# Exponentials of an attention block on GpSimd: one block of 256 per unit by a power, beside VectorE's polynomial

## The chip, the core and the metric

The kernel runs on one core of a Trainium2 chip. The metric is the device time of one execution in microseconds (us); the median of three runs before the change is 932.26 us (931.24 to 934.92). TensorE (PE) multiplies matrices, ScalarE (ACT) evaluates functions, VectorE (DVE) does arithmetic on tiles, GpSimd (POOL) is a slower processor for tiles, and SyncE (SP) issues most DMAs.

## What is computed

```
x = A_x                                           # 1 x 2048 x 1024, bf16
g = sigmoid((x * gate_w).sum(-1))
a = 2 Re(C h) + x * Dskip,   h_t = Lam_bar h_(t-1) + B_bar x_t      # 1024 complex states, 2048 steps
q, k, v = x @ wqkv                                # 32 heads of 32
b = softmax(q k^T / sqrt(32)) v @ wo              # no mask, 2048 x 2048 scores a head
out = g * a + (1 - g) * b
```

## The kernel before, in words

**The attention loop sets the order of all work.** The 32 heads go in 8 groups of four, the 2048 queries in 8 blocks of 256; a group with a block is a *unit* (64 in all, g and qb of `normalize`, L1707). A unit has 8 *bursts*, each of which takes two tiles of 128 keys. So there are 512 bursts, counted by p in the loop of `build` (L1781). A burst has 8 score matmuls (L1615), which fill two slots of two PSUM banks (128 x 1024 scores each), and two exponentials, one for each slot (`exp` in `burst`, L1626). The probabilities lie in the tiles `pt` (and, early, in others that are free: the names f_cT, f_OT, f_Et in the profile) and are multiplied with V some bursts later (`pv`, L1684: 16 matmuls of 33 columns a burst, all accumulated in one PSUM bank with a column of ones, which gives the sum of the softmax). At the end of a unit `normalize` takes the reciprocal of the sums and scales.

**Everything else is fitted into the gaps by a planner that runs when the program is built.** Each burst has a place for four dense matmuls of 512 columns (`MM_PER_PERIOD`, L1847 on): projections for the next group (`d_qk`, `d_v`), the input of the state-space part (`d_u`), its output (`d_c`) and the output projection (`d_out`). They go through PSUM bank 7, and VectorE empties it (`evac`) after each chain of eight or so. VectorE's own work stands in lists: tables (`table_ops`), the folding of C (`fold_ops`) and, above all, the 32 items of the recurrence (`item_ops`, L1335: products, two scans of 512 steps, products). The planner holds a model of VectorE's clock, `dve_t`, adds to it a fixed price for each operation (0.61 us for a product, 1.24 for a scan, 0.735 for a step of the polynomial) and puts an operation into a burst if it ends in time. The order of every engine's queue is fixed by this; at run time only semaphores hold things back, and each engine takes its queue in order.

**The polynomial.** ScalarE alone would do 16 exponentials of 1024 columns a unit. For the bursts named in `X_PLAN` and `X_AT` (L935, L936), 256 of the 2048 exponentials of a burst (head 4 of the second key tile, the last 256 columns of the second slot) are done on VectorE instead: `x_in` (L1624) scales the scores from PSUM into `xi` as whole numbers, and the second exponential of that burst, which waits for it (`deps=[first]`, L1632), then has 768 columns (L1631). Two such blocks make a *pair*: when the second is in, three operations on 512 columns evaluate the polynomial (`x_ops`, L1658, L1659, L1655), GpSimd turns the result into the bits of a bf16 (L1656) into `xp`, and `x_pv` (L1667) multiplies it with V, 7 or 9 bursts after the start of the unit. With two pairs a unit, four of its eight bursts have a short exponential. Before the change this is so from burst 112 (unit 14) to 507, but for bursts 320 to 327 and 332 to 351.

GpSimd has little else: for each item it copies the last state (`hl`, L1358, behind the second scan), and three times it carries the state over (`carry`, L1385).

**Buffers.** `wb` holds the weights of two groups for q, k and v and three tiles of B; the `wo` rows come into the same places when these are no longer used.

Of the kernel before, what the change touches and what calls it, by code (L numbers as in the profile page):

```python
# [6 lines left out]
BF = mybir.dt.bfloat16  # L7
# [926 lines left out]

X_AT = ((0, 2), (4, 6))  # L935
X_PLAN = (112, 116, 120, 124, 128, 132, 136, 140, 144, 148, 152, 156, 160, 164, 168, 172, 176, 180, 184, 188, 192, 196, 200, 204, 208, 212, 216, 220, 224, 228, 232, 236, 240, 244, 248, 252, 256, 260, 264, 268, 272, 276, 280, 284, 288, 292, 296, 300, 304, 308, 312, 316, 328, 352, 356, 360, 364, 368, 372, 376, 380, 384, 388, 392, 396, 400, 404, 408, 412, 416, 420, 424, 428, 432, 436, 440, 444, 448, 452, 456, 460, 464, 468, 472, 476, 480, 484, 488, 492, 496, 500, 504)  # L936
X_COLS = 256
# [21 lines left out]
class FastPath:  # L959

    def __init__(self, nc, S, es, d, flag):
# [10 lines left out]
        self.V = T("V", [128, 2, 16, 4, 33], BF)  # L972
        wb = T("wb", [128, 9216], BF)
        self.w = wb[:, 0:6144].rearrange("p (s q a n) -> p s q a n", s=2, q=3, a=8)
        self.bT = wb[:, 6144:9216].rearrange("p (s a n) -> p s a n", s=3, a=8)

        row = lambda o, n: wb[:, o:o + 1024 * n].rearrange("p (a n) -> p a n", a=n)
        self.wo3 = [row(0, 3), row(6144, 3), row(3072, 1), self.cT[0][:, 0:1, :]]
        self.wo = [(self.wo3[0][:, a, :], "wo0") for a in range(3)] + [(self.wo3[1][:, a, :], "wo1") for a in range(3)]
        self.wo += [(self.wo3[3][:, 0, :], "wo3"), (self.wo3[2][:, 0, :], "wo2")]  # L980
# [4 lines left out]
        self.hp = hp  # L985
        self.hpx = wb[:, 6144:9216].rearrange("p (k n) -> p k n", k=6)
        ub = T("ub", [128, 2, 2, 512], BF)
# [70 lines left out]
    def ld_x(self, i, eng="sp"):  # L1058

        for r, n in ((0, 128), (1, 128)) if i == 0 else ((2 * i, 256),):  # L1060
            self.dma(lambda e, r=r, n=n: e.dma_start_transpose(self.xT[:, :, 128 * r:128 * r + n], self.x2[128 * r:128 * r + n, :]),  # L1061
                     [], [("xr", r + k) for k in range(n // 128)], "ld_x", eng)

    def ld_w(self, g, part, eng="sp"):
        cb = 1024 * part + 128 * g
        self.dma(lambda e: e.dma_start(self.w[:, g % 2, part], self.wsrc[:, :, cb:cb + 128]), [], [("w", g % 2, part)], "ld_w", eng)

# [12 lines left out]
    def begin(self):  # L1080
# [24 lines left out]
        pool(lambda e: e.tensor_copy(flat(24, 28), ioti), ["ioti"], ["iot"])  # L1105
        pool(lambda e: e.tensor_scalar(flat(28, 32), flat(24, 28), 16.0, 0.0, ALU.mult, ALU.add), ["iot"], ["ioth"])
        pool(lambda e: e.memset(self.V[:, :, :, :, 32:33], 1.0), [], ["v1"])
        pool(lambda e: e.memset(self.init[:], 0.0), [], ["init"])
# [13 lines left out]
    def piece(self, part, i, bank, first):  # L1122

        ps, w, xT = self.ps, self.w, self.xT
        for h in range(2):
            r = 2 * i + h

            def mm(e, r=r, h=h):
                m = None
                for a in range(8):  # L1130
                    m = e.matmul(ps[:, bank, 128 * h:128 * (h + 1)], w[:, 0, part, a, :], xT[:, a, 128 * r:128 * (r + 1)], start=(a == 0), stop=(a == 7))
                return m
            kw = dict(writes=[("bank", bank)]) if h == 0 else dict(acc=[("bank", bank)])
            yield lambda mm=mm, kw=kw, r=r: self.S.op("pe", mm, reads=[("w", 0, part), ("xr", r)], name="proj", **kw)

    def half256(self, part, i, half):
        ps, w, xT = self.ps, self.w, self.xT

        def mm(e):
            m = None  # L1140
            for a in range(4 * half, 4 * half + 4):
                m = e.matmul(ps[:, 7, 0:256], w[:, 0, part, a, :], xT[:, a, 256 * i:256 * (i + 1)], start=(a == 0), stop=(a == 7))
            return m
        self.S.op("pe", mm, reads=[("w", 0, part), ("xr", 2 * i), ("xr", 2 * i + 1)], name="proj", **(dict(acc=[("bank", 7)]) if half else dict(writes=[("bank", 7)])))

    def opening(self):
        S, ps, w, xT, dve = self.S, self.ps, self.w, self.xT, self.dve

# [265 lines left out]
    def d_qk(self, g, part, ch, bank=7):  # L1414
        ps, w, xT = self.ps, self.w, self.xT
        mms = []
        for a in range(8):
            mms.append((1, lambda e, f, l, a=a: e.matmul(ps[:, bank, :], w[:, g % 2, part, a, :], xT[:, a, 512 * ch:512 * (ch + 1)], start=f, stop=l),  # L1418
                        [("w", g % 2, part)] + self.xtok(ch)))
        if part == 0:  # L1420
            z = (4 * g + ch) % 5
            dst, tok = self.Q[:, z, :], ("Q", z)
        else:
            dst, tok = self.K[:, g % 2, 512 * ch:512 * (ch + 1)], ("K", g % 2, ch)
        return self.chain(mms, "proj", lambda: self.dve(lambda e: e.tensor_copy(dst, ps[:, bank, :]), [("bank", bank)], [tok], "evac_qk"), bank)  # L1425

    def d_v(self, g, f, bank=7):
        ps, w, xT = self.ps, self.w, self.xT
        mms = []
        for q in range(4):  # L1430
            kt = 4 * f + q
            for half in range(2):
                def fn(e, first, last, q=q, kt=kt, half=half):
                    m = None
                    for a in range(4 * half, 4 * half + 4):
                        m = e.matmul(ps[:, bank, 128 * q:128 * (q + 1)], xT[:, a, 128 * kt:128 * (kt + 1)], w[:, g % 2, 2, a, :],  # L1436
                                     start=(a == 0), stop=(a == 7))
                    return m
                mms.append((1, fn, [("w", g % 2, 2)] + self.xtok(f)))
        src = ps[:, bank, :].rearrange("p (k h c) -> p k h c", k=4, h=4)  # L1440
# [162 lines left out]
    def burst(self, B):  # L1603
# [17 lines left out]
        if mine is not None:  # L1621
            b, n = mine
            s = sl[1]
            first = self.dve(lambda e: e.tensor_scalar(self.xi[:, X_COLS * n:X_COLS * (n + 1)], ps[:, 2 * s + 1, 512 - X_COLS:512], X_A, X_LO, ALU.mult, ALU.max),  # L1624
                             [("S", s)], [("xi", n)], "x_in")
        def exp(z):  # L1626
            s, p = sl[z], self.pt_of(B, z)
# [16 lines left out]
    def x_ops(self, b):  # L1644
# [8 lines left out]
        def last():  # L1653
# [6 lines left out]
                (X_LAST, 0.0, last)]  # L1660

    def x_flush(self):
        c, wait, f = self.xbg.pop(0)
# [20 lines left out]
    def pv(self, q0, q1):  # L1684

        ps, V = self.ps, self.V
        for q in range(q0, q1):
# [6 lines left out]
            def mm(e, B=B, z=z, p=p, kl=kl, i=i, g=g):  # L1694
                m = None
                for h2 in range(1 if z == kl == 1 and B in self.x_of else 2):
                    for qt in range(2):
# [27 lines left out]
    def build(self):  # L1725
# [8 lines left out]
        for m in range(3):  # L1734
            self.ld_b(m)
        for part in (1, 2, 0):
            self.ld_w(1, part)
        self.plan()
        self.pt_own = {}
        self.x_of, self.x_batch, self.x_when = {}, [], {}  # L1740
        self.xbg, self.x_done, self.x_out = [], set(), 0
        self.opening()
# [38 lines left out]
        for p in range(first, NBURST):  # L1781
# [10 lines left out]
            period = PERIOD - (0.17 if p - 1 in self.x_of else 0.0)  # L1792
            if p in self.x_of:
# [28 lines left out]
            if pg == 25 and g + 2 < GROUPS:  # L1822
                assert g or not (proj[0] or cur and cur.tag == "proj")
                for part in (1, 2, 0):
                    self.ld_w(g + 2, part)
            wsv = self.d["B_wo"].rearrange("(a p) n -> p a n", p=128)
            if p == 386:
                self.dma(lambda e: e.dma_start(self.wo3[0], wsv[:, 0:3, :]), [], ["wo0"] + [("w", 0, q) for q in range(3)], "ld_wo")
            if not cs and cur is None and not wo1 and self.c_left[3] == 0:
                wo1 = True  # L1830
                self.dma(lambda e: e.dma_start(self.wo3[1], wsv[:, 3:6, :]), [], ["wo1"] + [("bT", r) for r in range(3)] + [("hp", 8, k) for k in range(6)], "ld_wo")
            if g >= 6 and not wo6 and not cs and self.c_left[3] == 0:
                wo6 = True
                self.dma(lambda e: e.dma_start(self.wo3[3], wsv[:, 6:7, :]), [], ["wo3", ("cT", 0, 0), ("cTf", 0, 0, 0), ("cTf", 0, 0, 1)], "ld_wo")
            if g >= 6 and not last and not proj[7] and not us and not cs and cur is None and not self.bg:

                last = True
                xs = [("xr", r) for r in range(16)]
                assert wo1 and wo6
                self.dma(lambda e: e.dma_start(self.wo3[2], wsv[:, 7:8, :]), [], ["wo2"] + [("w", 1, q) for q in range(3)] + xs, "ld_wo")  # L1840
            if g >= 6 and not cs and self.c_left[3] == 0 and nal < 8 and p > self.c_end:
# [280 lines left out]
```

## Time and profile before

| | us |
|---|---|
| median of 3 runs | 932.26 |
| lowest, highest | 931.24, 934.92 |
| the profiled execution, own time | 928.48 |
| its span in the profile | 926.7 |
| ACT busy in the span | 908.3 (98%) |
| PE busy | 883.7 (95%) |
| DVE busy | 758.9 (82%) |
| POOL busy | 74.4 (8%) |

The span lies within the execution's own time: 1.8 us are outside of it. The page of the profile gives busy times, a strip of 40 slices of the span (a digit is the busy share in tenths), the chain of work that ended last, and groups of instructions: line, engine, operation, written tile <- read tiles, shapes, how often, the busy time in us, the mean duration of one in ns, and then the idle time of the engine just before them. A window of the trace gives for each engine its busy time and in brackets the number of instructions that touch the window. A timeline gives the start in us, the time, and the instruction; xN stands for N in a row.

### The profile page before, as it was taken

The numbers are of one execution on the slowest core, as the hardware profiler recorded it, in microseconds if no ns is written. First come the engines' busy times: TensorE is split into PE (matmuls) and PEld (weight loads), VectorE is DVE, ScalarE is ACT, GpSimd is POOL, SyncE is SP. The second block draws the span as 40 slices with busy tenths as digits, with TensorE's granted clock in tenths as the row PEclk, the third lists the DMA queues.
The fourth block names the chain that finished last, engine by engine and source line by source line (L and its number), as shares of the span: only waits on it lengthen the run. The fifth ranks groups of instructions, "written<-read, shape, count | busy, mean of one in ns | idle before, by whom it ended". The sixth has DMA issues, their size and how long they took to land.

```text
span 926.7 us, 33866 instructions
## 1 busy us (share of the span) xinstructions
PE 883.7 (95%) x15095; PEld 502.8 (54%) x15316; DVE 758.9 (82%) x1310; ACT 908.3 (98%) x1034; POOL 74.4 (8%) x156
## 2 busy tenths in 40 slices
PE   8899999999999999999999999999999999989995
PEld 4555744447555565556655565555655655545553
DVE  2789989888989989889898989998998655676665
ACT  6999999999999999999999999999999999999997
POOL 2000000000100100102110100100010010001000
PEclk9999999999999999999999999999999999999999
DMA  9579737730114305572011511523002012424312
GB/s 205 93 127 167 115 80 137 156 86 16 42 53 102 70 20 102 120 160 52 19 51 53 122 38 27 120 64 102 19 17 65 21 48 74 145 85 123 118 63 75
DMA packets 170920, 77.71 MB, mean 84 GB/s; under 512 B 147216, under 2 KB 155408, under 8 KB 170768
## 3 DMA queue, kind: packets, MB, share of 16 engines
q1 hardware_dynamic: 168608, 74.94, 35.9%
q8 instruction: 121, 1.98, 0.9%
q10 hardware_dynamic: 2160, 0.53, 0.3%
q14 instruction: 31, 0.25, 0.1%
HBM read 25.18 MB, written 20.97 MB: 50 GB/s over the span
## 4 chain that ended last, share of the span: by engine, by line
PE 51%; ACT 36%; DVE 8%; issue 2%; DMA 1%; SPq 1%; DVEq 0%; ACTq 0%
ACT f_pt L1634 28%; PE f_ps L1700 11%; PE f_ps L1615 11%; PE f_ps L1495 8%; PE f_ps L1418 8%; PE f_ps L1448 6%; PE f_ps L1436 5%; ACT f_pt L1631 4%; DVE f_xi L1624 3%; ACT f_cT L1634 2%; ACT f_OT L1634 1%; ACT f_Et L1634 1%; SPq L1061 1%; PE f_ps L1679 1%; DMA f_xT<-in_A_x_dram 1%
## 5 line engine op out<-in xcount | busy, mean ns | idle before, releaser
L1634 ACT ACTIVATE f_pt<-f_ps 128x1024 bf16<-128x1024 f32 x760 | 727.7, 1113 | 1.2 <-PE f_ps L1615 1.0
L1700 PEld LDWEIGHTS f_ps<-f_V,f_pt 128*128 128x128 bf16 x7184 | 222.4, 96 | 94.8 <-issue 67.5
L1700 PE MATMUL f_ps<-f_V,f_pt 128*128 128x33 bf16 x7184 | 257.9, 178 | 0.3 <-ACT f_pt L1634 0.3
L1615 PE MATMUL f_ps<-f_Q,f_K 32*128 32x256 bf16 x4096 | 203.4, 273 | 14.4 <-ACT f_pt L1634 5.6
L1631 ACT ACTIVATE f_pt<-f_ps 128x768 bf16<-128x768 f32 x184 | 162.8, 885 | 3.0 <-DVE f_xi L1624 1.6
L1615 PEld LDWEIGHTS f_ps<-f_Q,f_K 32*128 32x128 bf16 x4096 | 60.8, 92 | 152.3 <-ACT f_pt L1634 125.4
L1448 PE MATMUL f_ps<-f_xT,f_wb 128*128 128x512 bf16 x448 | 117.7, 379 | 7.9 <-issue 2.3
L1418 PE MATMUL f_ps<-f_xT,f_wb 128*128 128x512 bf16 x406 | 106.7, 379 | 4.2 <-DVE f_K L1425 0.3
L1656 POOL TENSOR_SCALAR f_xp<-f_xq 128x512 int16<-128x512 f32 x92 | 57.3, 623 | 603.5 <-DVE f_xq L1655 385.9
L1624 DVE TENSOR_SCALAR f_xi<-f_ps 128x256 int32<-128x256 f32 x184 | 77.7, 423 | 19.5 <-PE f_ps L1615 13.7
L1355 DVE TENSOR_TENSOR_SCAN f_ht<-f_pf,f_init,f_ut 128x512 bf16<-128x512 f32 x64 | 79.7, 1272 | 0.0
L1495 PE MATMUL f_ps<-f_cT,f_hp 128*128 128x512 bf16 x240 | 67.6, 379 | 2.1
L1658 DVE SCALAR_TENSOR_TENSOR f_xq<-f_xi 128x512 f32<-128x512 uint16 x92 | 63.7, 692 | 3.1
L1659 DVE SCALAR_TENSOR_TENSOR f_xq<-f_xq,f_xi 128x512 f32<-128x512 f32 x92 | 63.6, 692 | 3.1
L1655 DVE SCALAR_TENSOR_TENSOR f_xq<-f_xi,f_xq 128x512 f32<-128x512 int16 x92 | 63.6, 691 | 2.7
L1448 PEld LDWEIGHTS f_ps<-f_xT,f_wb 128*128 128x128 bf16 x512 | 40.0, 96 | 40.6 <-issue 8.6
L1436 PE MATMUL f_ps<-f_wb,f_xT 128*128 128x128 bf16 x896 | 59.3, 219 | 0.0
L1526 PE MATMUL f_ps<-f_wb,f_OT 128*128 128x512 bf16 x186 | 55.0, 379 | 2.9 <-DVE f_Et L1538 0.9
L1418 PEld LDWEIGHTS f_ps<-f_xT,f_wb 128*128 128x128 bf16 x464 | 36.1, 96 | 35.4 <-issue 7.6
L1452 DVE CAST f_ub<-f_ps 128x512 bf16<-128x512 f32 x64 | 44.1, 689 | 11.8 <-PE f_ps L1448 9.2
L1436 PEld LDWEIGHTS f_ps<-f_wb,f_xT 128*128 128x128 bf16 x896 | 50.4, 97 | 3.8 <-issue 3.8
L1713 DVE RECIPROCAL f_rc<-f_ps 128x8 f32<-128x8 f32 x63 | 13.1, 207 | 44.2 <-PE f_ps L1679 35.7
(149 smaller groups left out, 797.7 us busy)
## 6 DMA issues: line engine op xcount, KB each, us to landing
u_scratch<-f_ub SPq DMA_DIRECT2D x64, 128.0 KB, 2.0
f_ub<-u_scratch SPq DMA_DIRECT2D x32, 256.0 KB, 2.8
ag_scratch<-f_Ag SPq DMA_DIRECT2D x32, 256.0 KB, 2.0
f_hp<-ag_scratch SPq DMA_DIRECT2D x32, 256.0 KB, 3.0
f_wb<-in_B_wqkv_dram SPq DMA_DIRECT2D x21, 256.0 KB, 4.2
out_dram<-f_xT SPq DMA_DIRECT2D x16, 256.0 KB, 2.0
f_wb<-in_B_wo_dram SPq DMA_DIRECT2D x2, 768.0 KB
f_OT<-f_On SPq DMA_TRANSPOSE x63, 2.3
```

Of the source, the lines that this page charges most:

```text
L1355: ops.append((1.24, lambda ri=ri: dve(lambda e: e.tensor_tensor_scan(ht[:, ri, :], rr, ut[:, ri, :], self.init[:, ri, j:j + 1], ALU.mult, ...
L1418: mms.append((1, lambda e, f, l, a=a: e.matmul(ps[:, bank, :], w[:, g % 2, part, a, :], xT[:, a, 512 * ch:512 * (ch + 1)], start=f, stop=l ...
L1436: m = e.matmul(ps[:, bank, 128 * q:128 * (q + 1)], xT[:, a, 128 * kt:128 * (kt + 1)], w[:, g % 2, 2, a, :], start=(a == 0), stop=(a == 7))
L1448: mms.append((1, lambda e, f, l, a=a: e.matmul(ps[:, 7, :], bT[:, (2 * n + ri) % 3, a, :], xT[:, a, 512 * ch:512 * (ch + 1)], start=f, sto ...
L1495: mms.append((1, lambda e, f, l, j=j, ri=ri, h=h: e.matmul(ps[:, 7, :], h[:, cols], cT[ri][:, j, 512 * cb:512 * (cb + 1)], start=f, stop=l ...
L1615: m = e.matmul(ps[:, 2 * sl[h // 2] + h % 2, 256 * kl:256 * (kl + 1)], K[32 * h:32 * h + 32, g % 2, 128 * kt:128 * (kt + 1)], Q[32 * h:32 ...
L1624: first = self.dve(lambda e: e.tensor_scalar(self.xi[:, X_COLS * n:X_COLS * (n + 1)], ps[:, 2 * s + 1, 512 - X_COLS:512], X_A, X_LO, ALU.m ...
L1631: self.S.op("act", lambda e: e.activation(flat(self.tile[p]), flat(ps[:, 2 * s:2 * s + 2, :]), ACT.Exp, scale=SCALE), reads=[("S", s)], wr ...
L1634: self.act(lambda e: e.activation(self.tile[p], ps[:, 2 * s:2 * s + 2, :], ACT.Exp, scale=SCALE), [("S", s)], [("pt", p)], "exp")
L1655: self.dve(lambda e: e.scalar_tensor_tensor(xq[:], hi, 128.0 / X_K, xq[:], ALU.mult, ALU.add), i2 + ["xq"], ["xq"], "x_q")
L1658: return [(0.73, 0.0, lambda: self.dve(lambda e: e.scalar_tensor_tensor(xq[:], lo, E2 / E3 * w, lo, ALU.add, ALU.mult), i2, ["xq"], "x_q") ...
L1700: m = e.matmul(ps[:, 6, o:o + 33], self.tile[p][:, h2, 256 * kl + 128 * qt:256 * kl + 128 * (qt + 1)], V[:, g % 2, 2 * i + kl, h, :], star ...
```

## The change

For units 8 to 49 (bursts 64 to 399) a unit has one polynomial pair, at its bursts 2 and 4, and one block of a new kind, at its burst 0. Units 50 to 63 keep two pairs. So units 8 to 13, which had none, now have three short exponentials each, and most of the units from 14 to 49 have three where they had four. The number of blocks goes from 184 to 42 + 138 = 180.

For the new block VectorE copies the 256 scores of each partition from PSUM, scaled to the base 2 and held above -126, as f32 into `yf` (`y_in`; the second exponential of the burst waits for it, and then has 768 columns). GpSimd raises 2 to these powers in four instructions of 64 columns (`y_pow`, tensor_tensor with a broadcast column of twos), which are put into its queue at bursts 0, 2, 4 and 6 of the unit. All four need only `yf`; the next unit's `y_in` needs all four to have read it. The result `yp` has two places, and `y_pv` multiplies it with V nine bursts after the start of the unit, ahead of the second exponential of that burst.

To find room in SBUF for `yf` and `yp`, the weights for q have one place for all groups instead of two: their load moves from the place pg 25 of the group before the last to pg 28 of the group before, and their four projections come at pg 32 or later. The rows of `wo` are spread over five loads instead of four.

```diff
-X_AT = ((0, 2), (4, 6))
-X_PLAN = (112, 116, 120, 124,
...
+X_AT = ((0, 2), (4, 6), (2, 4))
+Y_COLS = 64
+Y_PLAN = (64, 72, 80, 88, 96,
...
+X_PLAN = (64, 72, 80, 88, 96,
...
-        wb = T("wb", [128, 9216], BF)
+        wb = T("wb", [128, 8192], BF)
+        self.wq = wb[:, 0:1024].rearrange("p (a n) -> p a n", a=8)
...
+        self.yf = T("yf", [128, X_COLS], F32)
+        self.yp = T("yp", [128, 2, X_COLS], BF)
...
+        if B in self.y_of:
+            s = sl[1]
+            first = self.dve(lambda e: e.tensor_scalar(self.yf[:], ps[:, 2 * s + 1, 512 - X_COLS:512], SCALE * math.log2(math.e), -126.0, ALU.mult, ALU.max),
+                             [("S", s)], ["yf"], "y_in")
...
+    def y_pow(self, s, k):
+        cols = slice(Y_COLS * k, Y_COLS * (k + 1))
+        self.pool(lambda e: e.tensor_tensor(self.yp[:, s, cols], self.pf[:, 33, 0:1].to_broadcast([128, Y_COLS]), self.yf[:, cols], ALU.pow),
+                  ["yf", "two"], [("yp", s, k)], "y_pow")
+
+    def y_pv(self, B):
+
+        ps, V = self.ps, self.V
+        U, i = divmod(B, BURSTS)
+        g = U // QUNITS
+
+        def mm(e):
+            m = None
+            for qt in range(2):
+                o = 33 * (4 * qt + 3)
+                m = e.matmul(ps[:, 6, o:o + 33], self.yp[:, U % 2, 128 * qt:128 * (qt + 1)], V[:, g % 2, 2 * i + 1, 3, :],
+                             start=False, stop=False, skip_group_check=True)
+            return m
+        self.S.op("pe", mm, reads=[("yp", U % 2, k) for k in range(X_COLS // Y_COLS)] + [("V", g % 2, i // 2), "v1"], acc=["O"], name="pvy")
...
-                proj[g][8 + c].after = 16 * c
+                proj[g][8 + c].after = max(16 * c, 32)
...
+            if p in Y_PLAN:
+                self.y_of.add(p)
             if p % 4 == 0 and p in X_PLAN:
-                self.x_plan(p // 8, X_AT[p // 4 % 2])
+                self.x_plan(p // 8, X_AT[2 if p in Y_PLAN else p // 4 % 2])
...
+            if p in self.y_of:
+                self.dve_t = max(self.dve_t, t0 + 0.45) + 0.4
+            if p % 8 // 2 * 2 * Y_COLS < 2 * X_COLS and p % 2 == 0 and p // 8 * 8 in self.y_of:
+                self.y_pow(p // 8 % 2, p % 8 // 2)
...
+                if p % 8 == 1 and p - 9 in self.y_of:
+                    self.y_pv(p - 9)
                 second()
...
+            if pg == 28 and g + 1 < GROUPS:
+                assert not (cur and cur.tag == "proj")
+                self.ld_w(g + 1, 0)
```

More of the change, by code (lines that the diff above doesn't have):

```diff
@@ L972, in __init__ @@
         self.V = T("V", [128, 2, 16, 4, 33], BF)
-        wb = T("wb", [128, 9216], BF)
-        self.w = wb[:, 0:6144].rearrange("p (s q a n) -> p s q a n", s=2, q=3, a=8)
-        self.bT = wb[:, 6144:9216].rearrange("p (s a n) -> p s a n", s=3, a=8)
+        wb = T("wb", [128, 8192], BF)
+        self.wq = wb[:, 0:1024].rearrange("p (a n) -> p a n", a=8)
+        self.wkv = wb[:, 1024:5120].rearrange("p (s q a n) -> p s q a n", s=2, q=2, a=8)
+        self.bT = wb[:, 5120:8192].rearrange("p (s a n) -> p s a n", s=3, a=8)
         row = lambda o, n: wb[:, o:o + 1024 * n].rearrange("p (a n) -> p a n", a=n)
-        self.wo3 = [row(0, 3), row(6144, 3), row(3072, 1), self.cT[0][:, 0:1, :]]
-        self.wo = [(self.wo3[0][:, a, :], "wo0") for a in range(3)] + [(self.wo3[1][:, a, :], "wo1") for a in range(3)]
+        self.wo3 = [row(1024, 2), row(5120, 3), row(3072, 1), self.cT[0][:, 0:1, :], self.cT[0][:, 1:2, :]]
+        self.wo = [(self.wo3[0][:, a, :], "wo0") for a in range(2)] + [(self.wo3[4][:, 0, :], "wo4")] + [(self.wo3[1][:, a, :], "wo1") for a in range(3)]
         self.wo += [(self.wo3[3][:, 0, :], "wo3"), (self.wo3[2][:, 0, :], "wo2")]
@@ L1062, in ld_x, with w_of @@
                      [], [("xr", r + k) for k in range(n // 128)], "ld_x", eng)
+    def w_of(self, g, part):
+        return (self.wkv[:, g % 2, part - 1], ("w", g % 2, part)) if part else (self.wq, ("w", 0, 0))
     def ld_w(self, g, part, eng="sp"):
         cb = 1024 * part + 128 * g
-        self.dma(lambda e: e.dma_start(self.w[:, g % 2, part], self.wsrc[:, :, cb:cb + 128]), [], [("w", g % 2, part)], "ld_w", eng)
+        w, tok = self.w_of(g, part)
+        self.dma(lambda e: e.dma_start(w, self.wsrc[:, :, cb:cb + 128]), [], [tok], "ld_w", eng)
     def ld_b(self, m):
@@ L1106, in begin @@
         pool(lambda e: e.tensor_scalar(flat(28, 32), flat(24, 28), 16.0, 0.0, ALU.mult, ALU.add), ["iot"], ["ioth"])
+        pool(lambda e: e.memset(self.pf[:, 33, 0:1], 2.0), [], ["two"])
         pool(lambda e: e.memset(self.V[:, :, :, :, 32:33], 1.0), [], ["v1"])
@@ L1122, in piece @@
     def piece(self, part, i, bank, first):
-        ps, w, xT = self.ps, self.w, self.xT
+        ps, xT = self.ps, self.xT
+        w = self.w_of(0, part)[0]
         for h in range(2):
@@ L1130, in mm @@
                 for a in range(8):
-                    m = e.matmul(ps[:, bank, 128 * h:128 * (h + 1)], w[:, 0, part, a, :], xT[:, a, 128 * r:128 * (r + 1)], start=(a == 0), stop=(a == 7))
+                    m = e.matmul(ps[:, bank, 128 * h:128 * (h + 1)], w[:, a, :], xT[:, a, 128 * r:128 * (r + 1)], start=(a == 0), stop=(a == 7))
                 return m
@@ L1136, in half256 @@
     def half256(self, part, i, half):
-        ps, w, xT = self.ps, self.w, self.xT
+        ps, xT = self.ps, self.xT
+        w = self.w_of(0, part)[0]
         def mm(e):
@@ L1141, in mm @@
             for a in range(4 * half, 4 * half + 4):
-                m = e.matmul(ps[:, 7, 0:256], w[:, 0, part, a, :], xT[:, a, 256 * i:256 * (i + 1)], start=(a == 0), stop=(a == 7))
+                m = e.matmul(ps[:, 7, 0:256], w[:, a, :], xT[:, a, 256 * i:256 * (i + 1)], start=(a == 0), stop=(a == 7))
             return m
@@ L1146, in opening @@
     def opening(self):
[L1147 removed]
+        S, ps, xT, dve = self.S, self.ps, self.xT, self.dve
         def evac(dst, bank, tok, first, eng=dve):
@@ L1414, in d_qk @@
     def d_qk(self, g, part, ch, bank=7):
-        ps, w, xT = self.ps, self.w, self.xT
+        ps, xT = self.ps, self.xT
+        w, tok = self.w_of(g, part)
         mms = []
         for a in range(8):
-            mms.append((1, lambda e, f, l, a=a: e.matmul(ps[:, bank, :], w[:, g % 2, part, a, :], xT[:, a, 512 * ch:512 * (ch + 1)], start=f, stop=l),
-                        [("w", g % 2, part)] + self.xtok(ch)))
+            mms.append((1, lambda e, f, l, a=a, w=w: e.matmul(ps[:, bank, :], w[:, a, :], xT[:, a, 512 * ch:512 * (ch + 1)], start=f, stop=l),
+                        [tok] + self.xtok(ch)))
         if part == 0:
@@ L1427, in d_v @@
     def d_v(self, g, f, bank=7):
-        ps, w, xT = self.ps, self.w, self.xT
+        ps, xT = self.ps, self.xT
+        w, wtok = self.w_of(g, 2)
         mms = []
@@ L1695, in mm @@
                 m = None
-                for h2 in range(1 if z == kl == 1 and B in self.x_of else 2):
+                for h2 in range(1 if z == kl == 1 and (B in self.x_of or B in self.y_of) else 2):
                     for qt in range(2):
@@ L1735, in build @@
             self.ld_b(m)
-        for part in (1, 2, 0):
+        for part in (1, 2):
             self.ld_w(1, part)
@@ L1740, in build @@
         self.x_of, self.x_batch, self.x_when = {}, [], {}
+        self.y_of = set()
         self.xbg, self.x_done, self.x_out = [], set(), 0
@@ L1791, in build @@
             second = self.burst(p)
-            period = PERIOD - (0.17 if p - 1 in self.x_of else 0.0)
+            period = PERIOD - (0.17 if p - 1 in self.x_of or p - 1 in self.y_of else 0.0)
+            if p in self.y_of:
+                self.dve_t = max(self.dve_t, t0 + 0.45) + 0.4
+            if p % 8 // 2 * 2 * Y_COLS < 2 * X_COLS and p % 2 == 0 and p // 8 * 8 in self.y_of:
+                self.y_pow(p // 8 % 2, p % 8 // 2)
             if p in self.x_of:
@@ L1823, in build @@
                 assert g or not (proj[0] or cur and cur.tag == "proj")
-                for part in (1, 2, 0):
+                for part in (1, 2):
                     self.ld_w(g + 2, part)
+            if pg == 28 and g + 1 < GROUPS:
+                assert not (cur and cur.tag == "proj")
+                self.ld_w(g + 1, 0)
             wsv = self.d["B_wo"].rearrange("(a p) n -> p a n", p=128)
             if p == 386:
-                self.dma(lambda e: e.dma_start(self.wo3[0], wsv[:, 0:3, :]), [], ["wo0"] + [("w", 0, q) for q in range(3)], "ld_wo")
+                self.dma(lambda e: e.dma_start(self.wo3[0], wsv[:, 0:2, :]), [], ["wo0"] + [("w", 0, q) for q in (1, 2)], "ld_wo")
             if not cs and cur is None and not wo1 and self.c_left[3] == 0:
@@ L1839, in build @@
                 assert wo1 and wo6
-                self.dma(lambda e: e.dma_start(self.wo3[2], wsv[:, 7:8, :]), [], ["wo2"] + [("w", 1, q) for q in range(3)] + xs, "ld_wo")
+                self.dma(lambda e: e.dma_start(self.wo3[2], wsv[:, 7:8, :]), [], ["wo2"] + [("w", 1, q) for q in (1, 2)] + xs, "ld_wo")
             if g >= 6 and not cs and self.c_left[3] == 0 and nal < 8 and p > self.c_end:
```

10 lines of the change are left out of this document (6 added, 4 removed).

## The prediction

> **What bounds the kernel now.** I read the busy shares first, then the chain, then what one exponential costs, then windows by stage.
>
> ```profile
> span 926.7 us, 33866 instructions
> PE 883.7 (95%) x15095; PEld 502.8 (54%) x15316; DVE 758.9 (82%) x1310; ACT 908.3 (98%) x1034; POOL 74.4 (8%) x156
> ...
> DVE  2789989888989989889898989998998655676665
> ...
> PE 51%; ACT 36%; DVE 8%; issue 2%; DMA 1%; SPq 1%; DVEq 0%; ACTq 0%
> ```
>
> ScalarE is busy 98% of the span, TensorE 95%, and the chain runs through both: two engines in lockstep. VectorE is at 8 to 9 tenths for the first two thirds and falls to 6 behind that. GpSimd is nearly idle.
>
> The unit of time is a unit of 8 bursts, 16 exponentials. Windows laid from the first exponential of a unit to that of another show the rate: units 12 and 13 (no short exponential), 24 and 25 (eight short ones), unit 9, and all units that the change touches, 8 to 49.
>
> ```profile
> core 0: us, PE busy (x) PEld busy (x) DVE busy (x) ACT busy (x) POOL busy (x), PEclk, DMA share, GB/s
> 187.63:216.95 29.32, 27.79 (x495) 16.39 (x499) 24.21 (x28) 29.32 (x34) 0.00 (x0) 1.00 0.23 52
> 357.07:384.68 27.61, 26.95 (x446) 14.20 (x452) 24.94 (x43) 27.61 (x33) 2.64 (x6) 1.00 0.66 134
> 143.90:158.35 14.45, 13.64 (x225) 7.04 (x226) 14.06 (x21) 14.45 (x17) 0.71 (x1) 1.00 0.69 129
> 129.05:722.10 593.05, 575.78 (x9890) 328.26 (x10033) 534.05 (x859) 590.27 (x673) 51.19 (x103) 1.00 0.32 73
> ```
>
> ACT is busy for the whole of the first two, so ScalarE sets their pace: 29.32 / 2 = 14.66 us a unit without blocks, 27.61 / 2 = 13.81 with four. One block is worth (14.66 - 13.81) / 4 = 0.21 us. TensorE needs 26.95 / 2 = 13.5 us in the faster units, so three blocks (14.66 - 0.64 = 14.02 us) are not TensorE's limit. The granted clock is 1.00 throughout, so the clock explains none of it.
>
> **The change, part by part.** *ScalarE.* 42 units at 14.02 us are 588.8 us where the trace has 593.05: a gain of 4.2 us, most of it from units 8 to 13, which get three blocks each; the later units lose the fourth, and this is made good only if the stalls that they now have go too. Units 50 to 63 are as they were. So without any new wait the span is 926.7 - 4.2 = 922.5 us.
>
> *VectorE.* In these 42 units it has now 65 pairs, after the change 42.
>
> ```profile
> L1355 DVE TENSOR_TENSOR_SCAN f_ht<-f_pf,f_init,f_ut 128x512 bf16<-128x512 f32 x56 | 69.8, 1272 | 0.0
> L1624 DVE TENSOR_SCALAR f_xi<-f_ps 128x256 int32<-128x256 f32 x130 | 54.9, 423 | 11.3 <-PE f_ps L1615 6.5 <-PE f_ps L1495 0.5
> L1658 DVE SCALAR_TENSOR_TENSOR f_xq<-f_xi 128x512 f32<-128x512 uint16 x65 | 45.0, 692 | 2.2
> L1659 DVE SCALAR_TENSOR_TENSOR f_xq<-f_xq,f_xi 128x512 f32<-128x512 f32 x65 | 45.0, 692 | 2.2
> L1655 DVE SCALAR_TENSOR_TENSOR f_xq<-f_xi,f_xq 128x512 f32<-128x512 int16 x65 | 44.9, 690 | 1.8
> ...
> 129.05:722.10 593.05, 132.80 (x223) 1.00 0.32 73
> ```
>
> A pair is (54.9 + 45.0 + 45.0 + 44.9) / 65 = 2.92 us; 23 fewer take away 67.2 us. `y_in` has the shape of L1624, a third of an f32 copy from PSUM: 42 x 0.423 = 17.8 us come in. VectorE's busy time goes from 534.0 to 484.7 us, its idle time from 59 to 588.8 - 484.7 = 104 us, if nothing else slows it. (The last row above is the products of the recurrence, L1346, in the same window; it is used below.)
>
> *GpSimd and the port.* 168 instructions of 64 columns are new, and no row shows a power. What does show is that GpSimd and VectorE lock each other out:
>
> ```profile
> 252.72 0.62 POOL L1656 TENSOR_SCALAR f_xp<-f_xq 128x512 int16<-128x512 f32 x1 [7.52 <-DVE f_xq L1655]
> ...
> 252.74 0.42 DVE L1624 TENSOR_SCALAR f_xi<-f_ps 128x256 int32<-128x256 f32 x1
> 253.08 0.79 DVE L1346 TENSOR_TENSOR f_ut<-f_ht,f_tq 128x512 f32<-128x512 bf16 x1
> ...
> 315.73 0.62 POOL L1656 TENSOR_SCALAR f_xp<-f_xq 128x512 int16<-128x512 f32 x1 [7.15 <-PE f_ps L1700]
> ...
> 315.91 0.97 DVE L1346 TENSOR_TENSOR f_ut<-f_ht,f_tq 128x512 f32<-128x512 bf16 x1
> ...
> 250.68 0.69 DVE L1346 TENSOR_TENSOR f_ut<-f_ht,f_tq 128x512 f32<-128x512 bf16 x1
> ...
> 580.57 1.15 POOL L1656 TENSOR_SCALAR f_xp<-f_xq 128x512 int16<-128x512 f32 x1 [3.73 <-PE f_ps L1679]
> ...
> 581.16 1.10 DVE L1346 TENSOR_TENSOR f_ut<-f_ht,f_Et 128x1024 bf16<-128x1024 bf16 x1
> ```
>
> A product of two SBUF tiles takes 0.69 us alone (at 250.68). Begun while GpSimd works, it takes 0.79 and 0.97 us, and in both cases it ends 0.53 us after GpSimd's end (253.34 and 316.35): it waits to the end of GpSimd's instruction. At 580.57 GpSimd is the one that waits (1.15 for 0.62 us), and the next product of VectorE then waits for it in turn and loses 1.10 - 0.69 = 0.4 us of the 0.62. The instructions take turns, and VectorE loses GpSimd's time less 0.2 us. Evacuations from PSUM run beside GpSimd undisturbed (L1624 began at 252.74 and took 0.42).
>
> The Trainium skill (SBUF — State Buffer, Who interferes with whom) states that the loser blocks fully for the whole of the other's instruction, and a VectorE operation with two SBUF inputs loses only to a GpSimd instruction that reads SBUF; the power reads two operands, so by that rule it locks like L1656, however long it takes.
>
> So two numbers decide: how long a power takes, and how often VectorE stands at such an operation. For the second: products 132.8, scans 69.8, polynomial 42 x 2.07 = 87 and the folds
>
> ```profile
> L1311 DVE TENSOR_SCALAR f_OT<-f_cT,f_pf 128x2048 f32<-128x2048 bf16 x8 | 10.3, 1282 | 0.1
> L1312 DVE SCALAR_TENSOR_TENSOR f_cT<-f_cT,f_pf,f_OT 128x1024 bf16<-128x1024 bf16 x8 | 10.2, 1279 | 0.1
> L1313 DVE SCALAR_TENSOR_TENSOR f_cT<-f_cT,f_pf,f_OT 128x1024 bf16<-128x1024 bf16 x8 | 10.2, 1277 | 0.0
> ```
>
> with 30.7: 320 of 484.7 us, 66%. For the first the nearest rows are
>
> ```profile
> L1656 POOL TENSOR_SCALAR f_xp<-f_xq 128x512 int16<-128x512 f32 x92 | 57.3, 623 | 603.5 <-DVE f_xq L1655 385.9 <-PE f_ps L1679 187.2 <-PE f_ps L1495 16.1
> L1389 POOL TENSOR_TENSOR f_cm<-f_hl,f_W 128x8 f32<-128x8 f32 x12 | 2.7, 260 | 0.3
> ```
>
> A two-input instruction costs 0.26 us with hardly any columns, and a pass of two operations costs at most 0.62 / 512 = 1.2 ns a column. Lower end: the power is one pass, 0.26 + 64 x 0.0012 = 0.34 us. But a power is a logarithm, a product and an exponential; this kernel's exponential alone is five passes of two operations (L1624, three of `x_ops`, L1656). With as many for the logarithm it is ten or eleven passes: 0.26 + 11 x 64 x 0.0012 = 1.1 us, an estimate from these two rows, which I take. Upper end: 25 passes, for special cases and a full f32 result, 2.2 us.
>
> The Trainium skill (GPSIMD Engine Reference, Elementwise — side-by-side cycle accounting) gives 2.6 cycles of 1.2 GHz an element for a two-input add; an estimate from that is 64 x 2.2 ns = 0.14 us, 0.40 us with the 0.26 of the row, and by it the sum would be that of the first rival. It prices no power.
>
> **The sum.** A power of 1.1 us that meets a product, a scan or a polynomial step (66%) costs VectorE 1.1 - 0.2 = 0.9 us; one that meets an evacuation or idle time (34%) I count half, since the next operation soon arrives: 0.66 x 0.9 + 0.34 x 0.45 = 0.75 us, times 168 = 125 us. VectorE then needs 484.7 + 125 = 610 us in a stretch of 588.8. Its densest unit now is 14.06 / 14.45 = 97% busy; at 97% it takes 629 us, 36 us more than 593.05. The four powers of a unit depend only on `yf`, so they run one behind another as the queue allows, in its first half, where the polynomial's inputs are that the exponentials wait for: ScalarE and TensorE stall, since a late evacuation holds bank 7 and a late `x_in` or `y_in` holds the second exponential. Behind the powers in GpSimd's in-order queue stand L1656 and the copies of L1358; the latter holds the next item's first product, the former `x_pv`, with some bursts in hand at 1.1 us.
>
> The span becomes 926.7 + 36 = 963 us, the profiled execution 928.48 + 36 = 964.5. The median of the runs shown lies 3.8 us above the profiled one, so the forecast is **968 us**.
>
> *The rest.*
>
> ```profile
> f_wb<-in_B_wqkv_dram SPq DMA_DIRECT2D x21, 256.0 KB, 4.2
> ```
>
> One more `wo` load and the seven moved loads of q weights count as nothing: a load lands after 4.2 us, and four bursts, 7.0 us at 14.02 a unit, lie between its issue at pg 28 and the first use at 32, with TensorE at other chains. If this cover is gone (a load queued behind others on SP), a projection waits the excess, at most the 4.2 us again, at each of 7 groups. The matmuls of `y_pv` replace two of `pv`. They wait for all four powers: at 1.1 us they are done by burst 6 of 9; at over 3 us TensorE would stand there.
>
> **Rivals.** *The power is short (or doesn't hold the port).* For: one row of 0.26 us and the idle GpSimd. Against: the passes counted above. If VectorE's time with the blocking is below 97% of 588.8, that is 571 us, there are 86 us for 168 powers, 0.51 each, which is 0.83 x (D - 0.2): it decides at D = 0.82 us. Below it nothing shows but the gain of ScalarE: 932.26 - 4.2 = 928 us, 0.45% below, not slower. *The power is long.* At D = 2.2 us it costs 0.83 x 2.0 = 1.66 a piece, 279 us; (484.7 + 279) / 0.97 = 787, so 194 us more: 1126 us. For: a full-precision power in software; against: nothing in the trace. *The change doesn't relieve what bounds.* Idle ScalarE between 129 and 722 us is 593.05 - 590.27 = 2.8 us now, so even a perfect version wins no more than its blocks; this is why the short power gives 928 and not less.
>
> **How the numbers follow.** Forecast (D from 0.95 to 1.7 us) 0.45; short power (below 0.82) 0.25, of which I put half beyond 0.5% faster, since 928 lies almost on that bound; around 0.9, a draw, 0.05; long (over 1.7) 0.25. A measurement of this kernel tells about 0.5% (4.7 us) from no change. So faster 0.12, same 0.18, slower 0.70. The range goes from 926, just under the clean case, to 1120, which holds D up to 2.15 us; I leave out some 0.15 above and 0.04 below. The likeliest case by itself reaches from 945 to 1060.
>
> **What would show it.** The mean of the power's row in GpSimd's groups (over or under 0.82 us); products and scans (L1346, L1355) longer than 0.69 and 1.27 us on the mean, by some 125 us in all; units 8 to 49 over or at 14.02 us; ACT idle in front of the short exponentials with the new `y_in` or `x_in` named as what ended it. It is wrong if products keep their length while powers run, if the power takes under 0.8 us, or if TensorE waits for `yp`.

## The result, and the profile after

The kernel takes **2183.85 us** (median of 4 runs, 2183.14 to 2186.18) where the kernel before takes 933.59 us (4 runs): 2.340 times as long, interval 2.334 to 2.346. The profiled span is 2181.3 us. That is far outside the forecast range; the direction was right, by luck as it turns out below, and the size was not.

The page of the kernel after, with its strip of 40 slices, its chain, its costliest groups:

```profile
span 2181.3 us, 33872 instructions
PE 971.8 (45%) x15095; PEld 530.0 (24%) x15316; DVE 707.7 (32%) x1237; ACT 919.9 (42%) x1034; POOL 1849.0 (85%) x302
...
ACT  8962432234223422342234323432243224336998
POOL 0059999999999999999999999999999999992000
PEclk9986676667666766676667766766667666768999
...
POOL 84%; PE 7%; ACT 6%; DVE 2%; issue 1%; SPq 0%; DMA 0%; DVEq 0%; ACTq 0%
POOL f_yp L1683 82%; ACT f_pt L1653 4%; PE f_ps L1739 2%; PE f_ps L1629 1%; PE f_ps L1509 1%; POOL f_xp L1675 1%; ACT f_pt L1650 1%; PE f_ps L1431 1%; PE f_ps L1450 1%; PE f_ps L1462 0%; SPq L1066 0%; DVE f_yf L1642 0%; ACT f_cT L1653 0%; DMA f_xT<-in_A_x_dram 0%; ACT f_Et L1653 0%
...
L1683 POOL TENSOR_TENSOR f_yp<-f_pf,f_yf 128x64 bf16<-128x64 f32 x168 | 1792.1, 10699 | 30.1 <-DVE f_yf L1642 27.4
...
L1650 ACT ACTIVATE f_pt<-f_ps 128x768 bf16<-128x768 f32 x180 | 150.8, 838 | 1173.2 <-DVE f_yf L1642 1172.4
L1718 PE MATMUL f_ps<-f_V,f_xp 128*128 128x33 bf16 x276 | 19.6, 190 | 927.1 <-POOL f_xp L1675 927.1
L1642 DVE TENSOR_SCALAR f_yf<-f_ps 128x256 f32<-128x256 f32 x42 | 17.8, 424 | 1165.9 <-POOL f_yp L1683 1165.9
```

Where ScalarE and TensorE stood in the chain, one line of GpSimd now is: L1683, the power, 82% of the span. 168 of them take 10.7 us each, 1792 us in all. ScalarE's work has hardly grown (919.9 us busy for 908.3), but it now stands idle for 1172 us in front of the short exponential, which waits for `y_in` (L1642); `y_in` in turn waits 1166 us for the powers of the unit before, since there is one `yf`. TensorE waits 927 us for `xp`, whose GpSimd instruction is behind the powers in the queue. These waits lie over one another; they aren't to be added.

The three stages, as windows, first before (the middle row of it stands in the prediction), then after; the middle one holds units 8 to 49:

```profile
0.00:129.05 129.05, 118.94 (x2045) 71.54 (x2066) 95.63 (x181) 120.87 (x134) 6.12 (x26) 1.00 0.78 130
...
722.10:926.70 204.60, 189.02 (x3170) 103.01 (x3225) 129.17 (x272) 197.17 (x229) 17.11 (x28) 0.99 0.27 85
```

```profile
0.00:131.07 131.07, 119.28 (x2045) 71.52 (x2066) 95.56 (x181) 120.95 (x134) 6.15 (x27) 1.00 0.74 126
131.07:1946.91 1815.84, 661.07 (x9895) 354.65 (x10038) 483.18 (x788) 601.72 (x673) 1796.88 (x245) 0.66 0.11 24
1946.91:2181.30 234.39, 191.48 (x3169) 103.82 (x3220) 128.94 (x270) 197.28 (x229) 45.95 (x31) 0.92 0.26 77
```

The middle stretch went from 593.05 to 1815.84 us, 43.2 us a unit, and GpSimd (the fifth busy time) is busy for 1796.88 of it, 99%: four powers of 10.7 us make 42.8 of a unit's 43.2 us. The last stage is 29.8 us longer, since unit 50 still waits for the last powers. The third busy time is VectorE's: 483.18 us. The prediction had 484.7 for its work alone and 125 more for a blocked port. The 125 aren't there.

One unit of the kernel after, GpSimd, then the two instructions of the next unit that wait. A timeline merges what follows directly: the first row holds the second and third power of a unit, the third row its fourth, and the last row the first two of the next unit.

```profile
803.02 21.15 POOL L1683 TENSOR_TENSOR f_yp<-f_pf,f_yf 128x64 bf16<-128x64 f32 x2
824.25 0.62 POOL L1675 TENSOR_SCALAR f_xp<-f_xq 128x512 int16<-128x512 f32 x1
824.95 10.52 POOL L1683 TENSOR_TENSOR f_yp<-f_pf,f_yf 128x64 bf16<-128x64 f32 x1
835.43 0.19 POOL L1370 CAST f_hl<-f_ht 128x2 f32<-128x2 bf16 x1
836.09 21.93 POOL L1683 TENSOR_TENSOR f_yp<-f_pf,f_yf 128x64 bf16<-128x64 f32 x2 [0.47 <-DVE f_yf L1642]
```

```profile
835.58 0.42 DVE L1642 TENSOR_SCALAR f_yf<-f_ps 128x256 f32<-128x256 f32 x1 [29.14 <-POOL f_yp L1683]
```

```profile
836.04 0.81 ACT L1650 ACTIVATE f_pt<-f_ps 128x768 bf16<-128x768 f32 x1 [28.46 <-DVE f_yf L1642]
```

The fourth power ends at 835.47; 0.1 us later `y_in` runs, after 29 us of nothing on VectorE, the short exponential follows at 836.04, the next first power at 836.09. GpSimd hardly stops; all others run one unit of about 14 us and then wait some 29.

### The profile page after: what moved, and what is told of

Same layout as the page of the kernel before. It is cut to its first block, busy times and chain, and to the rows that moved or that the text cites. A ratio compares the mean times of both kernels' runs of the same rounds, so it can differ in the third digit from the quotient of the medians.

```text
span 2181.3 us, 33872 instructions
## 1 busy us (share of the span) xinstructions
PE 971.8 (45%) x15095; PEld 530.0 (24%) x15316; DVE 707.7 (32%) x1237; ACT 919.9 (42%) x1034; POOL 1849.0 (85%) x302
## 4 chain that ended last, share of the span: by engine, by line
POOL 84%; PE 7%; ACT 6%; DVE 2%; issue 1%; SPq 0%; DMA 0%; DVEq 0%; ACTq 0%
POOL f_yp L1683 82%; ACT f_pt L1653 4%; PE f_ps L1739 2%; PE f_ps L1629 1%; PE f_ps L1509 1%; POOL f_xp L1675 1%; ACT f_pt L1650 1%; PE f_ps L1431 1%; PE f_ps L1450 1%; PE f_ps L1462 0%; SPq L1066 0%; DVE f_yf L1642 0%; ACT f_cT L1653 0%; DMA f_xT<-in_A_x_dram 0%; ACT f_Et L1653 0%
## 5 line engine op out<-in xcount | busy, mean ns | idle before, releaser
L1683 POOL TENSOR_TENSOR f_yp<-f_pf,f_yf 128x64 bf16<-128x64 f32 x168 | 1792.1, 10699 | 30.1 <-DVE f_yf L1642 27.4
L1650 ACT ACTIVATE f_pt<-f_ps 128x768 bf16<-128x768 f32 x180 | 150.8, 838 | 1173.2 <-DVE f_yf L1642 1172.4
L1718 PE MATMUL f_ps<-f_V,f_xp 128*128 128x33 bf16 x276 | 19.6, 190 | 927.1 <-POOL f_xp L1675 927.1
L1642 DVE TENSOR_SCALAR f_yf<-f_ps 128x256 f32<-128x256 f32 x42 | 17.8, 424 | 1165.9 <-POOL f_yp L1683 1165.9
L1718 PEld LDWEIGHTS f_ps<-f_V,f_xp 128*128 128x128 bf16 x276 | 12.7, 104 | 931.4 <-POOL f_xp L1675 931.4
L1629 PE MATMUL f_ps<-f_Q,f_K 32*128 32x256 bf16 x4096 | 216.6, 288 | 17.8 <-ACT f_pt L1653 10.2
L1675 POOL TENSOR_SCALAR f_xp<-f_xq 128x512 int16<-128x512 f32 x69 | 42.6, 618 | 176.0 <-PE f_ps L1718 83.0
L1462 PE MATMUL f_ps<-f_xT,f_wb 128*128 128x512 bf16 x448 | 136.1, 426 | 9.8 <-issue 5.1
L1431 PE MATMUL f_ps<-f_xT,f_wb 128*128 128x512 bf16 x406 | 122.1, 422 | 7.8 <-DVE f_K L1438 2.0
L1509 PE MATMUL f_ps<-f_cT,f_hp 128*128 128x512 bf16 x240 | 79.0, 430 | 3.2 <-issue 1.3
L1638 DVE TENSOR_SCALAR f_xi<-f_ps 128x256 int32<-128x256 f32 x138 | 58.1, 421 | 33.1 <-PE f_ps L1629 29.9
```

Source lines behind the costliest of these rows:

```text
L1431: mms.append((1, lambda e, f, l, a=a, w=w: e.matmul(ps[:, bank, :], w[:, a, :], xT[:, a, 512 * ch:512 * (ch + 1)], start=f, stop=l), [tok] ...
L1462: mms.append((1, lambda e, f, l, a=a: e.matmul(ps[:, 7, :], bT[:, (2 * n + ri) % 3, a, :], xT[:, a, 512 * ch:512 * (ch + 1)], start=f, sto ...
L1509: mms.append((1, lambda e, f, l, j=j, ri=ri, h=h: e.matmul(ps[:, 7, :], h[:, cols], cT[ri][:, j, 512 * cb:512 * (cb + 1)], start=f, stop=l ...
L1629: m = e.matmul(ps[:, 2 * sl[h // 2] + h % 2, 256 * kl:256 * (kl + 1)], K[32 * h:32 * h + 32, g % 2, 128 * kt:128 * (kt + 1)], Q[32 * h:32 ...
L1650: self.S.op("act", lambda e: e.activation(flat(self.tile[p]), flat(ps[:, 2 * s:2 * s + 2, :]), ACT.Exp, scale=SCALE), reads=[("S", s)], wr ...
L1675: self.pool(lambda e: e.tensor_scalar(bits, xq[:], X_K, 128.0 * (E0 + 126.0), ALU.mult, ALU.add), ["xq"], p2, "x_p")
```

## The experiments

**Theories.** T: the loss is GpSimd's time for 168 powers in a row; nothing else in the change costs much. Rivals: W, the new waits and queue order cost by themselves; P, the prediction's own, that a power holds VectorE's port as long as it runs; B, the single `yf` is what makes all wait, not the throughput. Each kernel below is the changed kernel with the edit shown.

### Products in place of powers

```diff
-... self.yf[:, cols], ALU.pow),
+... self.yf[:, cols], ALU.mult),
```

> The new block is not an exponential here: GpSimd multiplies by two in place of raising two to the power; queues, waits and sizes are those of the change. My theory (call it T: the time is that of 168 powers in a row on GpSimd, 10.7 us each in the profile after the change): without them the kernel is at the clean case of the prediction, 928 us, between 924 and 934; the instruction takes 0.3 to 0.5 us. Rival (call it W: the change's new waits and queue order cost much by themselves): over 945 us.

Measured: 930.43 us against 933.45, ratio 0.9965 (0.9942 to 0.9988).

```profile
L1683 POOL TENSOR_TENSOR f_yp<-f_pf,f_yf 128x64 bf16<-128x64 f32 x168 | 85.5, 530 | 104.6 <-DVE f_yf L1642 102.8
```

The same queues with the same instruction in the same shape, 0.53 us long on the mean instead of 10.7: the whole loss is gone, and W with it. What is left is the prediction's clean case: 0.45% forecast, 0.35% measured. In its profile ScalarE is busy for 591.48 of the 591.86 us of units 8 to 49, so a version with these same blocks can hardly win more.

### One power and three products

```diff
-... self.yf[:, cols], ALU.pow),
+... self.yf[:, cols], ALU.mult if k else ALU.pow),
```

> The first quarter of each block is a power, the other three are products with two, so three quarters of the block are not exponentials. GpSimd then has 10.5 + 3 x 0.4 + 0.6 = 12.3 us of work a unit of 14.0 us. T, with the port let go early: within 1% of the kernel with products alone, 925 to 940 us. The rival of the prediction (call it P: the power holds the port as long as it runs): VectorE loses about 10.3 us at 66% of 42 powers, some 285 us less its 104 us of idle time, over 1100 us; products on VectorE up to 10 us long.

Measured: 933.5 us against 933.45, ratio 0.9997 (0.9972 to 1.0022); 0.3% over the kernel with products alone. GpSimd computes powers for 42 x 10.5 = 441 us of a stretch of 594 us, and it costs about 3 us. Here is what GpSimd and then VectorE do in one of them (the x3 row is a power and two products; the power runs from 301.06 to 311.58):

```profile
301.06 12.15 POOL L1683 TENSOR_TENSOR f_yp<-f_pf,f_yf 128x64 bf16<-128x64 f32 x3
```

```profile
301.82 0.68 DVE L1358 TENSOR_TENSOR f_tq<-f_ub,f_Et 128x1024 bf16<-128x1024 bf16 x1
...
305.25 1.28 DVE L1367 TENSOR_TENSOR_SCAN f_ht<-f_pf,f_init,f_ut 128x512 bf16<-128x512 f32 x1
...
307.55 0.69 DVE L1677 SCALAR_TENSOR_TENSOR f_xq<-f_xi 128x512 f32<-128x512 uint16 x1
```

A product from two SBUF tiles (0.68 us), a scan (1.28) and a polynomial step (0.69) all run at their usual length while the power runs. Over all 42 powers, no product, scan, polynomial step or two-input fold that began more than 0.75 us into one and ended inside it was over 0.02 us longer than usual, and VectorE's busy time in the stretch is 484.53 us (488.13 with products alone). P falls: the power doesn't hold the port for its length.

### Powers of several sizes

```diff
+        n = (8, 16, 32, 0)[k]
+        for a, b, op in ((0, n, ALU.pow), (n, Y_COLS, ALU.mult)):
```

> Powers of 8, 16 and 32 columns in each block, products with two for the other 200 columns, so most of the block is not exponentials. T says nothing on this by itself; if the power's time goes by the column (167 ns each from 10.7 us for 64) they take 1.3, 2.7 and 5.3 us and the unit still fits: 925 to 940 us. If it is mostly a fixed price of an instruction they take near 10 us each, 30 us a unit, and the time is near 1600 us.

Measured: 930.08 us, one run.

```profile
L1686 POOL TENSOR_TENSOR f_yp<-f_pf,f_yf 128x16 bf16<-128x16 f32 x42 | 121.8, 2899 | 0.0
```

The power of 16 columns is nearly always undisturbed. That of 8 begins a unit and often waits at its start, and the group of 32 columns holds products too, so their means don't serve; the shortest record does. The shortest records are 1.63, 2.89, 5.41 us for 8, 16, 32 columns, and 10.52 for 64 in the kernel before this one: 0.157 to 0.160 us for each further column and 0.37 us for the instruction. So the power goes by the column; there is no large fixed price that larger pieces would save. Why a column takes so long, no run shows.

### Two places for the scaled copy

```diff
-        self.yf = T("yf", [128, X_COLS], F32)
+        self.yf = T("yf", [128, 2, X_COLS], BF)
```

> The scaled copy has two places (in bf16, so that they fit), so a unit's copy no longer waits for the powers of the unit before, but for those two units before. T: four powers, 4 x 10.6 + 1.3 = 43.9 us, still set the unit, 2150 to 2200 us. Rival (call it B: the single buffer is what costs, since the wait for it is 1166 us in the profile): under 1500 us.

Measured: 2156.25 us, one run. The copy is bf16 here, so that two fit, and a power takes 10.59 us on the mean. The wait that is longest in the profile after, the short exponential's for `y_in`, is down from 1172 to 37.6 us, and the time is nearly as before; B falls. What the waits of this kernel (waiting instruction <- what it waits for, us in all, times, longest) show is that others take its place:

```profile
ACT f_pt L1653 <- PE f_ps L1629: 1179.5, 86, 30.5
...
PEld f_ps L1718 <- POOL f_xp L1675: 917.8, 42, 29.8
```

ScalarE waits as long as before, 1180 us, now for scores that TensorE hasn't made, because TensorE stands in front of `xp`, which GpSimd has behind its powers. A long wait at the top of the list is where the shortage comes out, not what it is.

### A middle dose: powers on 24 columns

```diff
+        for a, b, op in ((0, 24, ALU.pow), (24, Y_COLS, ALU.mult)):
```

> Each of the four instructions of a unit is a power on 24 columns and a product with two on the other 40, so five eighths of the block are not exponentials. From the powers of 16, 32 and 64 columns (2.89, 5.41, 10.52 us) a power costs 0.37 + 0.158 us a column, here 4.16 us. GpSimd has 4 x 4.16 + 4 x 0.3 + 0.6 + about 0.5 = 19 us a unit where ScalarE needs 14.0. T: the unit is GpSimd's, 42 x 19 = 798 us for 593, and the time is 1135 us, between 1100 and 1170. If instead something else than GpSimd's queue were behind the loss (the wait for one buffer, the order of matmuls), it would be near 930 or over 1500.

Measured: 1169.19 us, one run, at the upper end of what T gave; span 1167.4.

```profile
L1684 POOL TENSOR_TENSOR f_yp<-f_pf,f_yf 128x24 bf16<-128x24 f32 x168 | 728.7, 4337 | 30.1 <-DVE f_yf L1642 27.4
L1684 POOL TENSOR_TENSOR f_yp<-f_pf,f_yf 128x40 bf16<-128x40 f32 x168 | 55.3, 329 | 0.0
```

A power of 24 columns takes 4.34 us on the mean (4.16 by the line; some wait for the port at their start). With the product beside each, and `xp`, a unit of GpSimd's work is (728.7 + 55.3) / 42 + 0.6 = 19.3 us, some 5 us over ScalarE's 14.0; (1167.4 - 926.7) / 42 = 5.7 us a unit is what the kernel lost. So the time follows GpSimd's queue as soon as it is longer than a unit.

### The block in every second unit

```diff
-Y_PLAN = (64, 72, 80, 88, ...
+Y_PLAN = tuple(range(64, 400, 16))
...
-                self.x_plan(p // 8, X_AT[2 if p in Y_PLAN else p // 4 % 2])
+                self.x_plan(p // 8, X_AT[2 if p < 400 else p // 4 % 2])
```

> The new block stands in every second unit from 8 to 48 alone, 21 instead of 42; the others have the one polynomial pair. By GpSimd's throughput alone (two units take as long as four powers, 44 us): 21 x 44 = 924 us for 42 units, 1260 us in all. By the deadline (the block's matmul nine bursts after the start waits 43 us, and only then come the seven bursts that are left to the next block, 12.4 us): 21 x 55.7 = 1170 us, 1500 us in all. T as I state it now is the second.

Measured: 1558.48 us, one run. Two units from burst 128 on:

```profile
364.90:378.89 13.99, 13.46 (x224) 7.09 (x225) 11.33 (x17) 13.99 (x18) 13.67 (x2) 1.00 0.57 119
378.89:423.02 44.13, 14.94 (x230) 7.61 (x231) 10.74 (x16) 14.48 (x17) 31.88 (x5) 0.69 0.18 38
```

```profile
365.22 43.35 POOL L1683 TENSOR_TENSOR f_yp<-f_pf,f_yf 128x64 bf16<-128x64 f32 x4 [4.15 <-DVE f_yf L1642]
408.65 0.62 POOL L1675 TENSOR_SCALAR f_xp<-f_xq 128x512 int16<-128x512 f32 x1
```

The unit with the block runs at full pace, 13.99 us; the next stands for 30 us, since the matmuls of the block and of the pair come at its second burst and GpSimd is done only at 409. The 43 us are not spread over two units, for the deadline is nine bursts, and GpSimd rests in what is left. The second reading (1500 us) was nearer, the throughput alone (1260) wrong; I had the pair at 55.7 us, it is 58.1.

### One power of 256 columns

```diff
-Y_COLS = 64
+Y_COLS = 256
```

> One power of 256 columns in place of four of 64. By the line through the sizes it takes 0.37 + 256 x 0.158 = 40.9 us, the unit 42.3 us, and the kernel 2110 us: cutting into four costs no more than three fixed prices. On the port: if the power fetches all its operands at its start, VectorE's two-input operations that begin later than about 1 us into it keep their length; if it holds the port throughout, they are up to 40 us long and the time is the same or longer.

Measured: 2126.24 us, one run (2110 expected), 41.4 us a power. Cutting it into four costs some 1.4 us a unit and is not the trouble. GpSimd, then VectorE, at the start of one:

```profile
1282.10 0.62 POOL L1675 TENSOR_SCALAR f_xp<-f_xq 128x512 int16<-128x512 f32 x1
1282.80 41.43 POOL L1683 TENSOR_TENSOR f_yp<-f_pf,f_yf 128x256 bf16<-128x256 f32 x1
```

```profile
1282.46 0.79 DVE L1358 TENSOR_TENSOR f_ht<-f_ub,f_Et 128x1024 bf16<-128x1024 bf16 x1
1283.18 1.10 DVE L1358 TENSOR_TENSOR f_tq<-f_ub,f_Et 128x1024 bf16<-128x1024 bf16 x1
...
1285.82 0.68 DVE L1358 TENSOR_TENSOR f_ut<-f_ht,f_tq 128x512 f32<-128x512 bf16 x1
```

The power's record starts while VectorE is at a product (1282.46 to 1283.25), and it is 0.31 us longer than the undisturbed 41.12: it waits. The product that begins at 1283.18 then takes 1.10 us, 0.4 more than usual, as if the power had the port for a moment. The one at 1285.82, 3 us into the power, takes 0.68 again. With 64 columns, a quarter as many, the same place costs 0.1 us. That fits a power that fetches its operands at its start and then computes off the port; how it does so inside, no run shows.

### The change's other parts

`no_block` leaves the new block out and keeps the rest; `weights_only` keeps the moved weights alone, with the pairs of the kernel before:

```diff
-            if p in Y_PLAN:
-                self.y_of.add(p)
```

```diff
-Y_PLAN = (64, 72, 80, 88, ...
+Y_PLAN = ()
-X_PLAN = (64, 72, 80, 88, ...
+X_PLAN = (112, 116, 120, 124, ...
```

> The change without the new block: one polynomial pair a unit in units 8 to 49, weights moved as in the change. Two blocks a unit: 42 x (14.66 - 0.43) = 597.7 us for the stretch that took 593.05, so 937 us; between 933 and 941. If VectorE's load is a bound there, it is faster than that.

> The one place for the q weights, their later loads and projections, and the split of wo, with the polynomial pairs of the kernel before and no new block. I costed this at nothing: within 0.5% of the kernel before. If a projection waits for its weights in each of seven groups: up to 30 us more.

Measured against 930.41 us for the kernel before: 937.77 us without the block, ratio 1.0072 (1.0047 to 1.0097), and 930.53 us with the weights alone, ratio 1.0002 (0.9991 to 1.0014). The moved weights cost nothing, as costed. One pair in each of the 42 units (84 blocks where the kernel before has 130) costs 0.7%, and the new block, with products, brings that back and 0.35% more.

## Why the prediction was wrong, step by step

- **The ScalarE term held, within what can be measured.** 4.2 us were forecast for the blocks; the kernel with products is 0.35% (0.12 to 0.58) faster, 3.0 us between the medians, and a unit takes 591.86 / 42 = 14.09 us in its profile where 14.02 was worked out. The same price of a block gave 937 us for the kernel without the new one, and 937.77 came.
- **VectorE's own work held.** 484.7 us were forecast for the stretch, 483.18 measured.
- **The power's duration failed, and decided all.** I took 1.1 us from a count of passes at 1.2 ns a column and 2.2 us as the upper end; it is 10.52 undisturbed and 10.70 on the mean. A column costs 158 ns, some 130 times the 1.2 ns of one pass, while I had counted 11 passes, at most 25. The step rested on the assumption that GpSimd's power is a chain of such passes; no row said so, and the upper end should have been open. The rival with the long power stopped at 2.2 us for the same reason. (The sum has a smaller slip too: 66% is the share of VectorE's busy time; of the stretch of 588.8 us, idle time included, the 320 us are 54%, which makes 116 us of its 125.)
- **The port failed.** The rows showed that L1656 holds VectorE up to its own end. From these I took it for every GpSimd instruction, with the Trainium skill (SBUF — State Buffer, Who interferes with whom) behind it. Here the power shows another thing: VectorE's two-input operations keep their length inside of it, and only those that begin in its first three quarters of a microsecond lose anything. The Trainium skill's rule, that the loser is blocked for the whole of the other's instruction, agrees with the trace for a simple pass (the products of 0.79 and 0.97 us that the prediction shows) and does not for the power. So the forecast of 36 us had the right sign by luck, from a mechanism that isn't there.
- **The step that carried the loss was in the text as an aside**: "They wait for all four powers: at 1.1 us they are done by burst 6 of 9; at over 3 us TensorE would stand there." The mechanism is this one, together with the wait of `y_in`, at a price that I hadn't worked out: four powers, 42.8 us, against a unit of 14.0. Had I asked at which duration GpSimd itself becomes the bound ((14.0 - 0.6) / 4 = 3.3 us) and what lies above it, the rival would have read 42 x (4 D + 1) us and, at D = 10.7, near the measured 1816. Two of the signs of being wrong that the prediction names came: products kept their length while powers ran, and TensorE waited for `yp` (227 us).
- The moved q weights and `wo` loads cost nothing, as forecast (1.0002).

Shown by runs: that the power's length is the whole loss (products: none of it; 24 columns: 5.7 us a unit; 64: (2181.3 - 926.7) / 42 = 29.9), that it goes by the column, that it doesn't hold the port, that neither the single buffer nor the cut into four is more than a small part (28 and 58 us of the 1250 lost). Not tried: an exponential on GpSimd made of plain products and sums. By an estimate from the products, five passes of four pieces at 0.53 us would be 10.6 us of a unit's 14.0; what their turns at the port would cost VectorE is open, and by the kernel with products it could bring some 0.3% at best.

## What to carry to other kernels

An idle engine is a resource only at the speed of the operation that it is given; where no row of the trace has that operation, its price has no upper end, and one instruction of it, measured alone, is worth more than any estimate from neighbouring rows. Ask of each moved piece of work at which duration its new engine becomes the bound of the loop, and price what happens above that too. When a wait dominates the list, see whether its removal only moves it: two buffers for `yf` took over 1100 us of waiting off one line, and 1180 stood on another.

## What was not expected of the hardware

- GpSimd's tensor_tensor power took 0.37 us and 158 ns a column of 128 partitions (8 to 64 columns; 41.1 us for 256), where the same instruction as a product took 0.23 to 0.29 us for 32 to 64 columns undisturbed.
- A power left VectorE's two-input operations at their length, but for its start: those that began in its first 0.75 us lost up to 0.12 us with 64 columns and some 0.3 to 0.4 with 256, as if it fetched its operands first. A power that began while VectorE was at such an operation was mostly longer by about what was left of it (10.90 us where 0.52 us of a product were left). The longest, 12.27 us, was 1.75 over where 1.05 us were left; the rest of that isn't explained.
- TensorE's granted clock fell to 0.66 in the middle stretch (1.00 before), with TensorE busy 661 of 1816 us: a matmul of 512 columns (L1462) took 426 ns on the mean of the kernel instead of 379. It goes with the waits: in the kernel with the block in every second unit, the unit at full pace had 1.00 and the one that stood for 30 us 0.69. With GpSimd busy for 99% of the stretch, the slower matmuls hid in its time.
